# A new order table for a linear-attention and feed-forward kernel on one core

## The chip, the core and the metric

The kernel runs on one core of one Trainium2 chip. The core has five engines that work side by side, each through its own queue, strictly in order: TensorE (PE in the profile) multiplies matrices, VectorE (DVE) and ScalarE (ACT) do elementwise work, GpSimd (POOL) does slower elementwise work and issues the two weight loads, and the SyncE queue (SP) issues all other DMA transfers. The metric is the device time of one execution in microseconds (us). An instruction that waits for a semaphore holds up everything behind it on its engine.

## What is computed

The inputs are q, k, v and a complex decay a, each for 4 batches, 8 heads, 768 steps and 48 features, in float32. The attention part is a recurrence over time, cut here to what matters:

```python
scale = minimum(mag, 0.999) / (mag + 1e-06)          # mag = |a|
for t in range(S):
    S_re, S_im = ar*S_re - ai*S_im + outer(k[t], v[t]), ar*S_im + ai*S_re
    y[t] = q[t] @ S_re
```

The heads are then put side by side (384 features), and each of the 3072 rows goes through a layer norm with a gain, a product with a 384 x 1536 matrix, a ReLU, a product with a 1536 x 384 matrix, and is added to its input:

```python
xn = (x - mu) / sqrt(var + 1e-06) * g_ln
out = x + maximum(xn @ w_ch1, 0.0) @ w_ch2
```

## The kernel before, in words

Time is cut into chunks of 128 steps; two chunks make a pair. There are 24 chunks (n = 0 to 23) and 12 pairs (P = 0 to 11), three pairs to a batch. The recurrence is turned into matrix products: the cumulated logarithm of the decay and its cumulated angle come from products with triangular matrices, q and k are scaled and turned by them, and inside a chunk the result is a masked product.

For each pair, by the names that the code uses: `are`, `aim`, `k`, `q`, `vf` are loads on SP (lines 400 and 448). `ln`, `iv`, `r`, `r2`, `u`, `l`, `lc` make the log of the magnitude; `dec` is its cumulated sum on PE (line 484), and `e`, `en` its exponentials on ACT. `th`, `ph`, `sin`, `cos` (with `qt` or `abs`) do the same for the angle. `ke`, `qe` multiply k and q by the exponentials, in two chunks each (m = 0, 1), and `ks`, `qs` multiply them by cosine and sine (a = 0, 1); pair 0 is in two halves of the heads. `v` copies the values to bfloat16.

For each chunk: `kT`, `qT` turn ks and qs over on PE (eight transposes each, line 598) and `ksT`, `qsT` copy them from PSUM to SBUF on DVE or ACT; where the table gives `ksT` or `qsT` to SP (line 603) a DMA turns them over and the PE part is left out. `am` (line 621) is the masked product of both, `atm` applies the mask on DVE, `gm` and `G` carry the state, `y` is the chunk's output (lines 682 and 685), `bn` its mean and variance, `x` the centred row, `xtr` and `xT` turn it over (lines 719, and 725 for the DMA form), `xr` keeps it for the residual.

For each pair the feed-forward part: `mm1` (line 752, six half-groups of six matmuls of 256 columns), `relu`, then for each chunk `mm2` (line 776, three groups of four matmuls of 384 columns), `ot` or `oa` with `ot` for the scaling and residual, and `st` for the store. The weights come once: `wl.0` (line 365) and `wl.1` (line 367) are issued by POOL, and `wc` (line 381) multiplies the nine blocks of the first by the gain on DVE.

At the start, 71 matmuls named `warm` (lines 806 and 810) read a constant and their results are used by nobody. 15 `tab` operations load tables of ACT's functions.

The order of the work is written out by hand in one table, `PLAN`: each token is an operation, its engine (P, A, V, G, S) and, where it uses PSUM, the first of its eight banks. `Graph.run` emits the operations in that order, so the table fixes the order on every engine. A token may end in `@other`: then the operation also waits until `other` is done. The code calls this "turns at the shared port". Rings of buffers (`RINGS`) say how many pairs or chunks may be in flight of each tile.

Of the kernel before, what the change touches and what calls it, by code (L numbers as in the profile page):

```python
# [42 lines left out]
are.1.0:S ue:G are.0.0:S are.0.1:S pad.qs.1:G pad.ks.2:G aim.1.0:S ident:G car0.0:G pad.qs.2:G aim.0.0:S tab.log.0:A  # L43
ln.1.0:A uec:G aim.0.1:S qrow:G iv.1.0:A uth:V are.2.0:S zdec:G@uth ln.0.0:A car0.1:G@uth ln.0.1:A pick:G@uth iv.0.1:A
k.0.0:S pad.qs.0:G iv.0.0:A q.0.1:S r.1.0:V q.0.0:S r.0.1:V tab.trig.1:A th.1.0:A r.0.0:V r2.0.1:V th.0.1:A r2.1.0:V
vf.0.1:S th.0.0:A r2.0.0:V warm.w0:P0 warm.w1:P0 warm.w2:P0 warm.w3:P0 warm.w4:P0 warm.w5:P0 warm.w6:P0 warm.w7:P0
warm.w8:P0 warm.w9:P0 warm.w10:P0 warm.w11:P0 warm.w12:P0 warm.w13:P0 warm.w14:P0 warm.w15:P0 warm.w16:P0 warm.w17:P0
warm.w18:P0 warm.w19:P0 warm.w20:P0 warm.w21:P0 warm.w22:P0 warm.w23:P0 warm.w24:P0 warm.0:P0 warm.1:P0 warm.2:P0
ph.0.1:P0 pad.ks.0:G@r2.0.0 aim.2.0:S ph.0.0:P6 car.0.1:V0 mask:G@r2.0.0 car.0.0:V6 pad.ks.1:G@r2.0.0 k.0.1:S
warm.w25:P1 warm.3:P1 warm.4:P1 ph.1.0:P2 tab.log.2:A u.0.1:A u.0.0:A l.0.1:V k.1.1:S u.1.0:A l.0.0:V lc.0.1:V  # L50
ln.2.0:A car.1.0:V2 q.1.1:S warm.w26:P1 warm.w27:P1 warm.5:P1 warm.6:P1 dec.0.1:P1 lc.0.0:V l.1.0:V en.0.1:A1
warm.7:P4 dec.0.0:P7 e.0.1:A1 iv.2.0:A q.1.0:S lc.1.0:V qe.0.1.0:V warm.w28:P4 warm.w29:P4 warm.8:P4 warm.9:P4
warm.10:P4 dec.1.0:P4 en.0.0:A7 uthc:V vf.0.0:S e.0.0:A7 r.2.0:V e.1.0:A4 warm.11:P1 warm.12:P1 dps.0:P7 are.3.0:S
r2.2.0:V en.1.0:A4 ke.0.0.0:V u.2.0:A gln:S ke.0.1.0:V qe.0.0.0:V aim.3.0:S qe.1.0.1:V qe.1.0.0:V k.1.0:S l.2.0:V
tab.trig.3:A sin.0.0:A6 sin.0.1:A0 warm.w30:P1 warm.w31:P1 warm.w32:P1 warm.w33:P1 warm.13:P1 warm.14:P1@en.1.0
warm.w34:P1 warm.w35:P1 warm.w36:P1 warm.w37:P1 warm.15:P1 warm.16:P1@qe.0.0.0 warm.w38:P1 warm.w39:P1 warm.w40:P1
warm.17:P1 warm.18:P1 warm.19:P1 warm.20:P1 qt.0.0:P6 qs.0.0.1:V sin.1.0:A2 qt.0.1:P0 ks.0.0.1:V vf.1.1:S lc.2.0:V
# [11 lines left out]
rstd.1:G xT.3:V2 tab.log.6:A u.3.0:A ke.2.0.0:V mm1.1.0.1:P2 relu.0.0:A0 l.3.0:V mm1.1.1.0:P4 relu.0.2:A6 mm1.1.1.1:P4  # L69
ks.2.0.0:V lc.3.0:V mm1.1.2.1:P0 ks.2.0.1:V relu.1.1:A4 qe.2.0.0:V dec.3.0:P6 rstd.0:A qs.2.0.0:V mm1.1.0.0:P2  # L70
en.3.0:A6 qs.2.0.1:V kT.5:P4 vf.2.1:S e.3.0:A6 qT.4:P5 mm1.1.2.0:P0 ksT.5:A4 qsT.4:V5 qT.5:P6 are.5.0:S G.3:V
relu.1.2:A0 kT.4:P5 qsT.5:V6 mm2.0.0:P4 are.6.0:S ksT.4:V5 ln.4.0:A am.5:P6 mm2.0.1:P4 iv.4.0:A atm.5:V6 aim.5.0:S
mm2.0.2:P4 relu.1.0:A2 am.4:P0 r.4.0:V q.3.0:S mm2.1.0:P5 atm.4:V0 r2.4.0:A v.2:G@r.4.0 mm2.1.1:P5 q.3.1:S mm2.1.2:P5
xr.2:G@r.4.0 u.4.0:A ot.0:V4 mm2.2.0:P6 ln.5.0:A l.4.0:V st.0:S gm.4:P2 mm2.2.1:P6 iv.5.0:A G.4:V2 y.4:P0 lc.4.0:V
ln.6.0:A mm2.2.2:P6 xr.3:V k.3.0:S bn.4:V0 xr.1:G@xr.3 dec.4.0:P2 iv.6.0:A r.5.0:G@xr.3 k.3.1:S x.4:V0 y.5:P1 e.4.0:A2
dps.3:P4 bn.5:V1 xtr.4:P0 vf.3.1:S mm2.3.0:P7 oa.2:A6 xT.4:V0 en.4.0:A2 vf.3.0:S x.5:V1 mm2.3.1:P7 qe.3.0.0:G ot.1:V5
r2.5.0:A xtr.5:P0 k.4.1:S mm2.3.2:P7 rstd.2:G xT.5:V0 qe.3.0.1:V mm1.2.0.0:P0 u.5.0:A aim.6.0:S qs.3.0.0:V
mm1.2.0.1:P0 qs.3.0.1:V q.4.1:S mm1.2.2.1:P2 ke.3.0.0:V ot.3:V7 mm1.2.2.0:P2 k.4.0:S tab.trig.7:A th.4.0:A ke.3.0.1:V
qT.6:P5 relu.2.2:A2 ks.3.0.0:V ph.4.0:P6 q.4.0:S decc.3:V4 ks.3.0.1:V relu.2.0:A0 mm1.2.1.0:P2 l.5.0:V k.5.0:S kT.7:P4
abs.4.0:A6 qsT.6:V5 v.3:G@l.5.0 dps.4:P1 car.4.0:A6 kT.6:P0 vf.4.0:S ksT.7:V4 sin.4.0:A6 r.6.0:G@l.5.0 qT.7:P5  # L80
ksT.6:V0 mm1.2.1.1:P2 are.8.0:S decc.4:A1 qsT.7:V5 th.5.0:A am.6:P6 st.1:S gm.6:P4 relu.2.1:A2 ot.2:G ph.5.0:P0
atm.6:V6 are.7.0:S th.6.0:A ke.4.0.0:G am.7:P2 G.6:V4 y.6:P5 sin.5.0:A0 mm2.5.0:P6 atm.7:V2 ke.4.0.1:G vf.4.1:S
cos.4.0:A mm2.5.1:P6 qe.4.0.1:G bn.6:V5 mm2.5.2:P6 abs.5.0:A0 q.5.0:S ks.4.0.1:V y.7:P2 cos.5.0:A q.5.1:S lc.5.0:V
gm.7:P4 mm2.4.0:P7 ks.4.0.0:V x.6:A5 bn.7:V2 mm2.4.1:P7 xr.5:G@ks.4.0.0 r2.6.0:A aim.7.0:S G.7:V4 qe.4.0.0:G@ks.4.0.0
mm2.4.2:P7 x.7:V2 k.7.0:S dec.5.0:P0 qs.4.0.0:V xtr.6:P2 qs.4.0.1:V xtr.7:P3 st.2:S kT.9:P4 tab.log.8:A e.5.0:A0
xT.6:V2 v.4:G@qs.4.0.1 qT.8:P5 xT.7:V3 en.5.0:A0 ksT.9:V4 mm1.3.1.0:P2 ksT.8:S xr.4:V ln.7.0:A qT.9:P4 qsT.8:V5
qe.5.0.0:G@xr.4 mm1.3.1.1:P2 u.6.0:A qsT.9:V4 aim.8.0:S mm1.3.2.0:P0 relu.3.1:A2 l.6.0:V am.9:P4 st.3:S mm1.3.2.1:P0
iv.7.0:A k.5.1:S lc.6.0:V atm.9:V4 mm1.3.0.0:P2 qe.5.0.1:G@lc.6.0 ln.8.0:A mm1.3.0.1:P2 relu.3.2:A0 r.7.0:G@lc.6.0
ot.4:V7 dec.6.0:P4 vf.5.1:S ot.5:V6 relu.3.0:A2 gm.8:P7 ph.6.0:P0 G.8:V7 rstd.3:G vf.6.1:S en.6.0:A4 qs.5.0.1:V
am.8:P2 r2.7.0:V st.4:S e.6.0:A4 mm2.6.0:P6 qs.5.0.0:V iv.8.0:A mm2.6.1:P6 atm.8:V2 k.6.0:S xr.7:G@qs.5.0.0 mm2.6.2:P6  # L90
u.7.0:A xr.6:G@qs.5.0.0 vf.5.0:S abs.6.0:V0 r.8.0:G@qs.5.0.0 y.9:P4 y.8:P2 k.6.1:S bn.9:V4 mm2.7.0:P3 q.7.1:S bn.8:V2
gm.9:P7 tab.trig.9:A sin.6.0:A0 mm2.7.1:P3 ke.5.0.1:G gs.9:V7 are.9.0:S x.9:A4 mm2.7.2:P3 ot.6:V6 ke.5.0.0:G th.7.0:A
qT.11:P4 x.8:V2 st.6:S dps.6:P5 G.9:G cos.6.0:A car.6.0:V0 qT.10:P2 q.6.0:S qsT.11:V4 xtr.8:P6 ke.6.0.0:G xtr.9:P7
ph.7.0:P0 xT.8:A6 xT.9:V7 th.8.0:A qsT.10:V2 q.6.1:S mm1.4.1.1:P6 l.7.0:V decc.6:A5 car.7.0:A0 mm1.4.0.1:P4 abs.7.0:A0
ks.5.0.0:V mm1.4.0.0:P4 r2.8.0:V aim.9.0:S sin.7.0:A0 ks.5.0.1:V mm1.4.1.0:P6 relu.4.0:A4 lc.7.0:V kT.10:P1 ot.7:V3
q.7.0:S ke.6.0.1:G@lc.7.0 kT.11:P2 relu.4.1:A6 ksT.10:V1 k.7.1:S mm1.4.2.0:P4 ksT.11:V2 st.5:S am.10:P0 ks.6.0.1:V
am.11:P6 atm.10:V0 dec.7.0:P2 v.5:G@ks.6.0.1 tab.log.10:A rstd.4:A mm1.4.2.1:P4 ln.9.0:A vf.6.0:S xr.8:G@ks.6.0.1
# [749 lines left out]
```

## Time and profile before

| what | value |
|---|---|
| three runs | 187.19, 187.59, 187.84 us; median 187.59 |
| profiled execution: span from its first to its last instruction | 185.6 us |
| median of the runs less that span | 2.0 us |
| TensorE clock granted | full in all 40 slices |
| busy: PE, DVE, ACT, POOL | 177.0, 157.7, 154.6, 99.8 us |

The page gives no time of the profiled execution beside its span. In the profile a line such as `24.53 12.18 DMA w1b<-in_moe_w_ch_dram` is a piece of the chain that ended last: its start in us, its length, and what it was. In a timeline the columns are start, length, engine, line of the code, operation, output and inputs, shapes and count; in square brackets stands the idle time of the engine ahead of it and what ended it. In a list of groups the two numbers behind the bar are the busy time in us and the mean length of one in ns.

### The profile page before, as it was taken

Reading aid. Unit: us, or ns where it says so; the run is one execution under the profiler, and the core shown is the slowest. Engines: PE = TensorE matmul, PEld = TensorE weight load, DVE = VectorE, ACT = ScalarE, POOL = GpSimd, SP = SyncE. Lnnn points to the kernel's source line nnn. Section 1 sums busy time; section 2 is a strip of 40 time slices with the busy share of each in tenths; the row PEclk is TensorE's granted clock in tenths of the full one; section 3 lists DMA queues with packets and bytes.
Section 4 is the critical chain, followed back from the end, with each engine's and each line's share of the span. In section 5 each row is a group of like instructions: output and inputs, shape, how many; then the busy total and the mean of one; then the engine's idle time right before and its main releaser. Section 6 shows DMA issues by size and latency. Waiting matters only on the chain.

```text
span 185.6 us, 5131 instructions
## 1 busy us (share of the span) xinstructions
PE 177.0 (95%) x2029; PEld 139.0 (75%) x2029; DVE 157.7 (85%) x302; ACT 154.6 (83%) x218; POOL 99.8 (54%) x128
## 2 busy tenths in 40 slices
...
## 3 DMA queue, kind: packets, MB, share of 16 engines
...
## 4 chain that ended last, share of the span: by engine, by line
PE 59%; ACT 14%; DMA 10%; DVE 10%; issue 3%; SPq 2%; DVEq 0%
PE banks L752 22%; PE banks L776 19%; DMA w1b<-in_moe_w_ch_dram 7%; PE banks L598 4%; PE banks L621 4%; ACT L815 3%; PE banks L484 2%; DMA are<-in_a_re_dram 2%; DMA k<-in_k_dram 2%; ACT are L457 2%; PE banks L682 2%; DVE l L473 1%; ACT h L764 1%; PE banks L685 1%; ACT w L455 1%
## 5 line engine op out<-in xcount | busy, mean ns | idle before, releaser
L752 PE MATMUL banks<-xT,w1b 128*128 128x256 bf16 x432 | 52.7, 273 | 0.2
L776 PE MATMUL banks<-w2b,h 128*128 128x384 bf16 (+2 forms) x300 | 52.5, 319 | 0.0
L752 PEld LDWEIGHTS <-w1b 128*128 128x128 bf16 x432 | 45.8, 114 | 1.7 <-DVE w1b L381 0.4
L764 ACT ACTIVATE h<-banks 128x1024 bf16<-128x1024 f32 x33 | 32.8, 1022 | 8.3 <-PE banks L752 8.1
L776 PEld LDWEIGHTS <-h 128*128 128x128 bf16 x300 | 26.9, 97 | 14.1
L292 DVE TENSOR_TENSOR atm<-banks,mask 128x1024 bf16<-128x1024 f32 x24 | 28.9, 1218 | 1.9 <-PE banks L621 1.6
L815 ACT ACT_TABLE_LOAD x15 | 19.2, 1283 | 1.0 <-PEq L831 0.8
L292 POOL TENSOR_TENSOR ke<-k,en 128x384 bf16<-128x384 f32 x14 | 12.7, 916 | 8.3 <-DVE l L476 5.6
L292 POOL TENSOR_TENSOR qe<-q,e 128x384 bf16<-128x384 f32 x15 | 13.7, 916 | 6.1 <-DVE w1b L381 1.9
L292 POOL TENSOR_TENSOR ks<-ke,trig 128x768 bf16<-128x768 bf16 x7 | 11.4, 1643 | 6.4 <-PE banks L752 4.2
L621 PE MATMUL banks<-qsT,ksT 128*128 128x128 bf16 x192 | 14.6, 219 | 0.1
L410 POOL TENSOR_SCALAR v<-vf 128x768 bf16<-128x768 f32 x7 | 5.8, 831 | 16.0 <-DVE r L292 8.9
L810 PE MATMUL banks<-u_e 128*128 128x512 f16 x42 | 11.7, 418 | 2.2 <-POOL u_e L320 2.2
L292 POOL TENSOR_TENSOR r<-aim,are 128x768 f16<-128x768 f32 x7 | 12.7, 1817 | 1.9 <-ACT x L699 1.5
L709 POOL TENSOR_SCALAR xr<-x,mv 128x384 f32<-128x384 bf16 x16 | 9.3, 586 | 8.1 <-PE banks L752 3.3
L621 PEld LDWEIGHTS <-ksT 128*128 128x128 bf16 x192 | 12.0, 98 | 1.8 <-DVE ksT L289 0.5
L692 DVE BATCH_NORM_STATS2 stats<-banks 128x6 f32<-128x384 f32 x24 | 13.4, 556 | 0.1
L682 PE MATMUL banks<-v,atm 128*128 128x48 bf16 x192 | 12.1, 183 | 0.3 <-ACT x L699 0.2
L473 DVE SCALAR_TENSOR_TENSOR l<-r,w 128x768 f16<-128x768 f16 (+1 forms) x13 | 11.5, 892 | 0.9 <-ACT r L469 0.7
L791 DVE SCALAR_TENSOR_TENSOR ot<-banks,rstd,xr 128x384 f32<-128x384 f32 (+2 forms) x18 | 10.5, 590 | 2.0 <-PE banks L776 1.6
L455 ACT ACTIVATE w<-are 128x768 f32<-128x768 f32 (+1 forms) x13 | 10.2, 790 | 2.3 <-DMA are<-in_a_re_dram 2.3
L682 PEld LDWEIGHTS <-atm 128*128 128x128 bf16 x192 | 11.0, 96 | 1.2 <-DVE atm L292 0.2
...
## 6 DMA issues: line engine op xcount, KB each, us to landing
...
```

What stands on the lines that cost most here:

```text
L292: {"DVE": nc.vector, "POOL": nc.gpsimd}[eng(name)].tensor_tensor(**kw)
L455: add(f"ln.{X}", lambda S_=S_: act(out=S_("w"), in_=S_("are"), func=AF.Ln), needs=[f"are.{X}"], uses=[("are", P), ("w", P)])
L473: nc.vector.scalar_tensor_tensor(out=S_("l"), in0=S_("r2"), scalar=0.5, in1=S_("w"), op0=ALU.mult, op1=ALU.add)
L621: nc.tensor.matmul(ps[:, h], lhsT=T("ksT", n)[:, h], rhs=T("qsT", n)[:, h], start=True, stop=True)
L682: nc.tensor.matmul(ps[:, h], lhsT=T("atm", n)[:, h], rhs=T("v", P)[:, c, h], start=True, stop=nfirst)
L692: nc.vector.bn_stats(out=T("stats", n), in_=bank(f"y.{n}")[:, 0:DM])
L752: nc.tensor.matmul(ps[:, jj], lhsT=w1b[:, dc, ts(gi, JG * C)].rearrange("k (p j) -> k j p", j=JG)[:, jj], rhs=T("xT", P)[:, dc].rearrange( ...
L764: act(out=dst, in_=src, func=AF.Relu)
L776: nc.tensor.matmul(bank(f"o.{N}")[:, ws], lhsT=T("h", P)[:, j, ts(c, C)], rhs=w2b[:, j, ws], start=(j == 0), stop=(j == NJ - 1))
L791: nc.vector.scalar_tensor_tensor(out=o, in0=bank(f"o.{N}")[:, ws], scalar=T("rstd", P)[:, ds(c, 1)], in1=xs, op0=ALU.mult, op1=ALU.add)
L810: g.add(f"warm.w{i}", lambda i=i: nc.tensor.matmul(bank(f"warm.w{i}"), lhsT=u_e[:, 0, 0], rhs=u_e.rearrange("p c j t -> p (c j t)"), start ...
L815: g.add(f"tab.{nm}.{i}", lambda tab=tab: nc.scalar.preload_act_table_set(tab))
```

## The change

Only `PLAN` is replaced; no operation's code is touched. The new table holds the same computation with these differences, counted token by token:

- 90 operations that stand in both tables are on another engine. Of the elementwise multiplications, 8 `ke` and 4 `qe` go from DVE to POOL and 4 `qe` the other way; 5 `ks` go each way; 3 `qs` go to DVE. 2 `r` go from DVE to POOL; of `x`, 8 go from DVE to ACT and 3 back; the rest are single ones of `v`, `xr`, `G`, `r2`, `relu`, `xT`, `ksT`, `qsT`, `rstd`, `ot`, `abs`, `decc`. DVE has 266 operations for 275, POOL 116 for 107, ACT 210 for 209.
- `ksT.21` and `xT.21` are no longer DMA transposes; so `kT.21` (eight transposes) and `xtr.21` (three) come in on PE.
- 66 tokens have an `@` for 47.
- The order is new on every engine, SP's loads and the `warm` matmuls among it, and so are many banks. The number of `warm` matmuls and of table loads is the same. The PE operations that stand ahead of the first `mm1` are the same set.

The diff, cut to the rows around the first weight load and the first feed-forward products:

```diff
--- before.py
+++ after.py
@@ -40,105 +40,106 @@
 PLAN = """
-cos.0.0:A6 ks.0.1.1:V warm.21:P1 warm.22:P1 qt.1.0:P2 qs.1.0.1:V cos.0.1:A0 vf.1.0:S dps.1:P5 qs.0.1.1:V cos.1.0:A2
-dec.2.0:P0 ks.0.1.0:V k.2.1:S ks.0.0.0:V decc.0:A7 qs.0.1.0:V kT.0:P6 decc.1:A5 qs.0.0.0:V th.2.0:A qs.1.0.0:V
-wl.0:G@qs.0.0.0 qT.0:P2 q.2.1:S v.0:V qT.1:P3 ksT.0:A6 qsT.0:V2 qT.2:P4 ke.1.0.0:G@v.0 k.2.0:S kT.1:P5 qsT.1:A3
...
-xT.1:A7 wc.1.0:V qt.3.0:P0 wc.1.2:V cos.2.0:A2 wl.1:G@xT.1 vf.2.0:S wc.0.0:V mm1.0.1.0:P6 wc.0.1:V cos.3.0:A0 bn.2:V5
-y.3:P3 aim.4.0:S mm1.0.1.1:P6 wc.0.2:V x.2:A5 wc.2.1:V wc.2.2:V mm1.0.0.1:P0 wc.2.0:V relu.0.1:A6 bn.3:V3
-qe.2.0.1:G@wc.2.0 xtr.2:P2 mm1.0.0.0:P0 xT.2:V2 x.3:V3 ke.2.0.1:G@wc.2.0 mm1.0.2.1:P6 gs.3:V4 xtr.3:P2 mm1.0.2.0:P6
...
+qt.1.0:P2 cos.0.1:A1 qs.1.0.1:V warm.w29:P5 warm.w16:P4 cos.1.0:A2 qs.0.1.0:V dec.2.0:P0 q.2.1:S qs.0.0.0:V ks.0.0.0:V
+th.2.0:A qT.0:P4 qs.1.0.0:V warm.9:P3 ks.0.1.0:V warm.11:P6 qT.2:P5 qsT.0:A4 ks.0.0.1:V wl.0:G@ks.0.1.0 kT.0:P7
+qsT.2:V5 k.2.0:S qT.1:P4 ksT.0:V7 ke.1.0.0:G kT.1:P2 are.4.0:S qsT.1:V4 warm.24:P7 am.0:P6 v.0:G tab.log.4:A ln.3.0:A
...
+wc.1.2:V xtr.1:P6 gm.3:P4 wc.1.0:V xT.1:A6 qt.3.0:P0 wc.1.1:V cos.2.0:A2 wc.0.2:V mm1.0.1.1:P6 wc.0.0:V are.5.0:S
+wl.1:G@wc.0.2 bn.2:V5 cos.3.0:A0 mm1.0.1.0:P6 wc.0.1:V x.2:A5 y.3:P3 wc.2.0:V aim.5.0:S wc.2.2:V relu.0.1:A6 xtr.2:P2
+wc.2.1:V mm1.0.0.0:P0 ke.2.0.1:G@wc.2.2 bn.3:V3 are.6.0:S mm1.0.0.1:P0 gs.3:V4 qe.2.0.1:G@bn.3 x.3:V3 mm1.0.2.1:P6
...
 """
```

More of the change, by code (lines that the diff above doesn't have):

```diff
@@ L42 @@
 PLAN = """
[L43 to L57, printed above, removed]
@@ L68 @@
-qe.2.0.1:G@wc.2.0 xtr.2:P2 mm1.0.0.0:P0 xT.2:V2 x.3:V3 ke.2.0.1:G@wc.2.0 mm1.0.2.1:P6 gs.3:V4 xtr.3:P2 mm1.0.2.0:P6
[L69 to L97, printed above, removed]
@@ L98 @@
-atm.11:V6 y.10:P0 qe.6.0.0:G e.7.0:A2 mm2.9.0:P1 k.8.0:S bn.10:V0 en.7.0:A2 qe.6.0.1:G ph.8.0:P6 q.8.1:S relu.4.2:V4
-u.8.0:A ks.6.0.0:G mm2.9.1:P1 are.11.0:S iv.9.0:A gm.10:P2 mm2.9.2:P1 G.10:V2 abs.8.0:A6 mm2.8.0:P3 qs.6.0.0:V x.10:A0
-xr.9:V y.11:P2 qs.6.0.1:V mm2.8.1:P3 bn.11:V2 qsT.13:S r.9.0:G@qs.6.0.1 xtr.10:P0 mm2.8.2:P3 x.11:V2 tab.trig.11:A
-sin.8.0:A6 kT.13:P4 ot.9:V1 are.10.0:S xT.10:A0 xtr.11:P2 qT.12:P5 ke.7.0.0:G th.9.0:A xT.11:V2 kT.12:P0 ot.8:V3
-k.8.1:S mm1.5.0.1:P6 cos.7.0:A qe.7.0.0:G ksT.13:V4 mm1.5.0.0:P6 st.8:S ksT.12:V0 cos.8.0:A v.6:G qsT.12:V5
@@ L138 @@
[L138 to L141 removed]
+ue:G are.1.0:S are.0.0:S are.0.1:S uth:V aim.1.0:S warm.w17:P5 uec:G warm.25:P7 aim.0.1:S warm.1:P4 warm.w32:P2
+aim.0.0:S pick:G@uth warm.w13:P5 are.2.0:S warm.w33:P5 tab.log.0:A ln.1.0:A warm.18:P1 ident:G warm.w37:P7 ln.0.0:A
@@ new lines @@
+G.4:V6 mm2.1.0:P1 vf.3.0:S decc.3:V5 xr.1:G bn.4:V0 dec.4.0:P2 r.5.0:G ot.0:V4 y.5:P6 e.4.0:A2 mm2.3.0:P5 st.0:S
+bn.5:V6 en.4.0:A2 k.3.0:S mm2.2.2:P7 x.5:V6 k.4.1:S x.4:A0 mm2.1.1:P1 k.4.0:S xr.3:V oa.2:A7 r2.5.0:V mm2.1.2:P1
+vf.3.1:S ln.6.0:A qe.3.0.1:V xtr.4:P4 xtr.5:P2 qe.3.0.0:G@r2.5.0 u.5.0:A mm2.3.1:P5 xT.5:V2 xT.4:V4 aim.6.0:S
+mm2.3.2:P5 iv.6.0:A ot.1:V1 ke.3.0.1:V mm1.2.2.0:P2 q.4.0:S qs.3.0.1:V mm1.2.0.0:P0 l.5.0:V mm1.2.0.1:P0 tab.trig.7:A
+th.4.0:A qs.3.0.0:V mm1.2.2.1:P2 ke.3.0.0:G@l.5.0 ot.3:V5 relu.2.0:A0 ph.4.0:P6 st.3:S rstd.2:G@qs.3.0.0 lc.5.0:V
@@ new lines @@
+relu.2.2:A2 st.1:S ks.3.0.0:V qT.6:P4 q.4.1:S ks.3.0.1:V qT.7:P0 sin.4.0:A6 ot.2:G@ks.3.0.0 qsT.6:V4 mm1.2.1.1:P2
+car.4.0:A6 qsT.7:V0 kT.6:P5 ke.4.0.1:G abs.4.0:A6 st.2:S mm1.2.1.0:P2 k.5.1:S ksT.6:V5 th.5.0:A ke.4.0.0:G@qsT.6
+aim.7.0:S kT.7:P4 q.5.1:S am.6:P6 relu.2.1:A2 ksT.7:V4 v.3:G@qsT.7 ph.5.0:P0 are.7.0:S atm.6:V6 cos.4.0:A r.6.0:G
+gm.6:P4 am.7:P2 sin.5.0:A0 vf.4.0:S G.6:V4 dps.4:P5 mm2.5.0:P6 abs.5.0:A0 atm.7:V2 ks.4.0.0:G gm.7:P4 q.5.0:S
+decc.4:A5 mm2.4.0:P7 th.6.0:A G.7:V4 y.6:P2 are.8.0:S y.7:P5 r2.6.0:A bn.6:V2 dec.5.0:P0 xr.4:G@G.7 cos.5.0:A bn.7:V5
@@ new lines @@
+qe.4.0.1:G mm2.4.1:P7 vf.4.1:S x.6:V2 x.7:A5 mm2.5.1:P6 qe.4.0.0:V mm2.4.2:P7 ks.4.0.1:V xtr.6:P3 qs.4.0.1:V
+mm2.5.2:P6 qs.4.0.0:V tab.log.8:A u.6.0:A xtr.7:P2 kT.9:P4 xT.6:V3 e.5.0:A0 xT.7:V2 qT.8:P5 ot.4:V7 mm1.3.1.0:P2
+en.5.0:A0 ksT.9:V4 qe.5.0.1:G st.4:S mm1.3.1.1:P2 ksT.8:S ln.7.0:A qsT.8:V5 xr.5:G@ksT.9 qT.9:P7 relu.3.1:A2 l.6.0:V
+mm1.3.2.1:P0 q.6.1:S mm1.3.2.0:P0 iv.7.0:A aim.8.0:S qsT.9:V7 qe.5.0.0:G@l.6.0 mm1.3.0.0:P2 ot.5:V6 relu.3.2:A0
+am.9:P4 lc.6.0:V st.5:S xr.7:V mm1.3.0.1:P2 ln.8.0:A vf.5.0:S v.4:G@lc.6.0 atm.9:V4 k.6.0:S ph.6.0:P0 relu.3.0:A2
```

121 lines of the change are left out of this document (77 added, 44 removed).

## The prediction, made before the changed kernel ran

> **What bounds the kernel now.** I read the stages first (busy time by engine, then granted clock, DMA share, GB/s), then the chain that ended last, then the timelines around its joints.
>
> ```profile
> core 0: us, PE busy (x) PEld busy (x) DVE busy (x) ACT busy (x) POOL busy (x), PEclk, DMA share, GB/s
> 0.00:37.48 37.48, 32.63 (x317) 20.01 (x318) 28.70 (x58) 33.90 (x53) 18.74 (x40) 1.00 0.99 216
> 37.48:182.02 144.54, 144.34 (x1712) 118.97 (x1712) 128.61 (x244) 120.67 (x166) 81.02 (x89) 1.00 0.88 186
> 182.02:185.60 3.58, 0.00 (x0) 0.00 (x0) 0.35 (x1) 0.00 (x0) 0.00 (x0) 1.00 0.33 112
> ```
>
> ```profile
> 24.53 12.18 DMA w1b<-in_moe_w_ch_dram
> 36.81 0.20 DVE w1b L381
> 37.08 0.36 DVE w1b L381
> 37.48 0.89 PE banks L752 x6
> ...
> 46.53 0.89 PE banks L598 x16
> ...
> 129.20 0.29 PE banks L579 x8
> ...
> 173.30 0.17 PE banks L719 x3
> ...
> 174.12 3.96 PE banks L752 x36
> 178.07 3.94 PE banks L776 x36
> ```
>
> The span falls into three parts. Up to 37.48 the kernel waits for the first weights: the load w1b is issued at 24.53, lands 12.18 us later, is scaled, and the first `mm1` starts. From there PE is busy 144.34 of 144.54 us at full clock. Then 3.58 us of last output and store. So the middle part is PE's sum of work, and DVE (128.61) and ACT (120.67) are under it. Is that PE working, or PE waiting with a matmul open? I went through PE's timeline group by group (487 groups from 37.48 to 177.91) and compared the distance of starts with the steps that the chain shows, 3.96/36 = 0.110 us for an `mm1` matmul and 3.94 us for 24 full-width `mm2` ones. Only four holes above 0.1 us appear, 0.78 us in all; the largest is here:
>
> ```profile
> 117.02 0.36 PE L579 MATMUL banks<-ident,e 128*48 128x1 bf16 x8
> 117.49 0.84 PE L752 MATMUL banks<-xT,w1b 128*128 128x256 bf16 x6
> ```
>
> Eight such matmuls take 0.29 us where the next follows at once (129.20 in the chain); here the next starts after 0.47. **The middle part has 0.2 us (by busy time) to 0.8 us (by holes) to give, no more.** A new order of the same work can gain beyond that only by an earlier first `mm1`.
>
> **Part one, PE's own work.** The set of PE operations ahead of the first `mm1` is the same in both tables, so nothing moves out of the middle part. `kT.21` and `xtr.21` come into it: eight transposes at 0.89/16 = 0.056 us are 0.45, three are 0.17. Sum **+0.6 us**. Nothing hides it, since PE has no holes; the DMA transposes that go were hidden already.
>
> **Part two, the start.** Two things must be ready: w1b with its scaling, and `xT.0`, `xT.1`.
>
> ```profile
> 24.53 0.99 POOL L365 DMA_DIRECT2D w1b<-in_moe_w_ch_dram  x1 [12.65 <-DVE qs L292]
> 37.46 0.83 POOL L367 DMA_DIRECT2D w2b<-in_moe_w_ch_dram  x1 [1.79 <-ACT xT L287]
> ```
>
> ```profile
> w1b<-in_moe_w_ch_dram POOLq DMA_DIRECT2D x1, 1152.0 KB, 12.2
> w2b<-in_moe_w_ch_dram POOLq DMA_DIRECT2D x1, 1152.0 KB, 11.3
> ```
>
> ```profile
> 20.51 1.57 ACT L521 ACTIVATE trig<-banks 128x384 bf16<-128x384 int16 x3
> 21.96 1.60 ACT L532 ACTIVATE trig<-banks 128x384 bf16<-128x384 int16 x3
> ...
> 36.68 0.47 ACT L287 COPY xT<-banks 128x384 bf16<-128x384 bf16 x1
> ...
> 39.11 0.58 ACT L699 ACTIVATE x<-banks,mv 128x384 bf16<-128x384 f32 x1 [0.54 <-DVE mv L693]
> ```
>
> POOL issues the load when `qs.0.0.0` is done; the new table hangs it on `ks.0.1.0`. DVE gives `ke.0.0.0` and `qe.0.0.0` to POOL, but that does not carry through: the six sines and cosines of pairs 0 and 1 on ACT, 20.51 to about 23.5, stand behind an unbroken row of the same ACT work in both tables. After `cos.1.0`, the last, the new DVE order has `qs.1.0.0` (0.5 by the rows of its shape below, less the overlap with its neighbours) and `ks.0.1.0` (a half, 0.3), and the load goes at about 24.35: 0.2 us earlier. SP's loads of this time are the same ones with a few exchanged; those of pair 2 and the angles of pair 4 share the DMA engines with w1b as before. I take 12.18 again, so the first `mm1` starts at about 37.3. **-0.2 us.** Bounds: w1b as fast as w2b, 11.3, would give 0.9 more, but then `xT.1` ends first: walking DVE's new order (two copies for each of q and k, `atm.0`, `atm.1`, `ks.1.0.1`, `bn.0`, three copies, `G.1`, `atm.2`, `bn.1`) puts `xT.1`'s end at 36.65 for 37.15, so no more than 0.7 in all. The other way, 0.5 later if more of SP's loads get ahead of it.
>
> **Part three, the first feed-forward products.**
>
> ```profile
> 38.61 1.48 PE L752 MATMUL banks<-xT,w1b 128*128 128x256 bf16 x12
> ```
>
> Before, `y.3` stands between the first half-group (37.48, 6 x 0.110) and this row, so it takes 0.4. The new order puts `xtr.2` one half-group (0.65 us) closer to the start: after two half-groups and `y.3`, 1.3 + 0.4 us behind 37.3, at 39.0. It needs `x.2`, which is made behind the same five scalings of w1b and `bn.2` as before; its row ends at 39.69, moved with w1b to 39.5. PE waits 0.5 us, where this stage had one of the four holes, 0.2: **+0.3 us**, bounds 0 and 0.6. The second weight load hangs on the fourth scaling for `xT.1`, some 0.3 us later; the first `mm2` moves 0.9 us later by the PE operations counted between it and the first `mm1`, so the load stays covered by 0.6 us. If it took 12.2 us it would cost 0.3.
>
> **Part four, the moved operations.** They lie beside PE's work. From the groups of one shape:
>
> ```profile
> L292 POOL TENSOR_TENSOR r<-aim,are 128x768 f16<-128x768 f32 x7 | 12.7, 1817 | 1.9 <-ACT x L699 1.5 <-ACT are L457 0.3
> L292 POOL TENSOR_TENSOR ke<-k,en 128x384 bf16<-128x384 f32 x14 | 12.7, 916 | 8.3 <-DVE l L476 5.6 <-ACT r L469 1.8 <-ACT en L488 0.8
> L292 POOL TENSOR_TENSOR ks<-ke,trig 128x768 bf16<-128x768 bf16 x7 | 11.4, 1643 | 6.4 <-PE banks L752 4.2 <-issue 2.2
> L473 DVE SCALAR_TENSOR_TENSOR l<-r,w 128x768 f16<-128x768 f16 x11 | 10.5, 954 | 0.1
> L709 POOL TENSOR_SCALAR xr<-x,mv 128x384 f32<-128x384 bf16 x16 | 9.3, 586 | 8.1 <-PE banks L752 3.3 <-DVE xr L709 2.4 <-DVE ks L292 1.3
> L292 DVE TENSOR_TENSOR ks<-ke,trig 128x768 bf16<-128x768 bf16 x15 | 8.3, 554 | 0.0
> L410 POOL TENSOR_SCALAR v<-vf 128x768 bf16<-128x768 f32 x7 | 5.8, 831 | 16.0 <-DVE r L292 8.9 <-DVE l L473 4.4 <-DVE ks L292 1.4
> L476 DVE TENSOR_SCALAR l<-l 128x768 f16<-128x768 f16 x11 | 3.9, 354 | 0.1
> L709 DVE TENSOR_SCALAR xr<-x,mv 128x384 f32<-128x384 bf16 x8 | 3.3, 413 | 0.0
> L292 POOL TENSOR_TENSOR r<-r 128x768 f16<-128x768 f16 x1 | 1.5, 1457 | 0.0
> L292 POOL TENSOR_TENSOR G<-gt,dec 128x384 bf16<-128x384 f32 x2 | 1.7, 828 | 1.3 <-DVE gt L292 1.3
> ```
>
> DVE falls by some 6 us in the middle part and POOL rises by 11 of 144; neither sets the end, so this relief is worth nothing by itself. What counts is whether the two get in each other's way. POOL and DVE take turns:
>
> ```profile
> 102.03 1.81 POOL L292 TENSOR_TENSOR r<-aim,are 128x768 f16<-128x768 f32 x1 [1.55 <-ACT x L699]
> ...
> 105.56 0.83 POOL L410 TENSOR_SCALAR v<-vf 128x768 bf16<-128x768 f32 x1
> ```
>
> ```profile
> 101.34 0.55 DVE L292 TENSOR_TENSOR qs<-qe,trig 128x768 bf16<-128x768 bf16 x1
> ...
> 106.38 0.55 DVE L292 TENSOR_TENSOR qe<-q,e 128x384 bf16<-128x384 f32 x1
> ```
>
> While POOL works from 102.03 to 106.39, DVE does only operations that read PSUM or one small tile; its next product of two SBUF tiles starts at 106.38. In the whole trace none of DVE's products runs beside more than a sliver of a large POOL operation. So these operations share one turn. From the first `mm1` of pair 4 to that of pair 7 (about 90 to 130 us) I count what needs it. Before: POOL 11 `ke`/`qe`, 4 `ks`/`qs`, 2 `r`, 3 `v`, 4 `xr` = 25.1; DVE 13 products at 0.554 (`ks`, `qs`, `ke`, `qe`, `r2`), 4 `l`, 4 `lc`, 3 `xr` = 13.7; together 38.8, beside 39.9 us of PE work. After: POOL 11 `ke`/`qe`, 4 `ks`/`qs`, 3 `r`, 1 `r2`, 2 `v`, 5 `xr`, 2 `G` = 29.8; DVE 11 products, 3 `l`, 4 `lc` = 10.4; together 40.2, beside 39.6 of PE. Elsewhere the sum stays under PE's over any such length, but for some ten us after 60. So the turn is full there, and an operation that comes late finds no room. Cost between 0 (POOL's `xr`, `v` and `r` have slack) and 2.2 us (below); I take 0, as PE waited only 0.3 at the fullest places of before.
>
> The Trainium skill, SBUF — State Buffer, section "SBUF: two separate sides", states that DVE and GpSimd share one pair of SBUF ports as an exclusive lock held for the whole instruction, by which a DVE operation with two SBUF inputs fully blocks against a GpSimd one that reads SBUF. The trace agrees (106.38 against 106.39). By that rule the stage's load is the 40.2 above, without it DVE's busy time alone; it speaks against moving products to an engine that holds the lock 0.916 us for 0.55.
>
> **Sum.** 185.6 + 0.6 - 0.2 + 0.3 = 186.3 us of span. The median of the three runs, 187.59, is 2.0 above the profiled span; so **188.3 us**.
>
> **Rivals.** (A) The shared turn becomes the bound from 90 to 130. Before, 38.8 us of turns went into 40.4 us, so 1.6 were lost between turns. The same loss on 40.2 makes 41.8, 2.2 over PE's 39.6: 190.5 us. For: the count, and 66 waits on `@` for 47. Against: fewer hand-overs (48 operations for 49), and not every operation is urgent. It decides once turns and hand-overs exceed PE's work. (B) The end on the other side: the load w1b comes through faster. Then `xT.1` ends the start, 0.7 earlier, and if the 0.8 us of holes go too: 185.6 - 0.7 + 0.6 - 0.8 = 184.7, or 186.7 us; with only the start, 187.5. For: w2b took 11.3. Against: DMA share 0.99 up to 37.48, the same loads beside it. (C) The holes close (DVE has 6 us more room) and the rest cancels: 186.3 - 0.8 = 185.5, 187.5 us, no change. (D) The change does not do what it says: an order that bears scattered load landings finds no landing to bear, because no hole of PE ends on a load after 37.48. That speaks for C or the forecast, not for a gain.
>
> **How the numbers follow.** The forecast with its own range 187.7 to 189.2: 0.45. A: 0.17. B: 0.18. C and D with no change: 0.20. About 0.3% (0.56 us) is what a measurement of this kernel can tell from no change: under 187.03 is faster, over 188.15 slower. Faster: most of B, 0.17. Same: C, the rest of B and a quarter of the forecast, 0.32. Slower: the rest, 0.51. The range leaves out half of B's lower end and A's upper tail: 186.8 to 190.3.
>
> **What would show it.** Right: first `mm1` at 37.0 to 37.5; PE busy for all but about 1 us from there to the last `mm2`, in a stretch of about 145.3; 264 + 8 transposes at line 598; a hole ahead of `xtr.2` near 39. A would show as PE holes between 90 and 130 with POOL's products ahead of them. Wrong: a first `mm1` before 36.6, or a middle part under 144.5, which would mean that PE had waited inside busy time where I saw none.

## The result, and the profile after

The changed kernel takes **189.27 us** (median of 15 runs, 188.50 to 190.88), the kernel before 187.59 (15 runs, 186.99 to 189.60): a ratio of 1.0083 (95% interval 1.0054 to 1.0113), slower. Its profiled execution spans 187.3 us for 185.6. In the new file each line of code has a number one higher (`mm1` is L753).

The stages of the changed kernel, cut like those of before at the first `mm1` and the last `mm2` (span, then busy us of PE, PEld, DVE, ACT, POOL, then clock, DMA share, GB/s):

```profile
0.00:38.08 38.08, 32.47 (x318) 20.69 (x319) 28.06 (x58) 33.09 (x53) 20.18 (x40) 1.00 0.97 209
38.08:183.62 145.54, 144.59 (x1724) 119.74 (x1723) 126.73 (x236) 122.22 (x167) 94.81 (x97) 1.00 0.87 184
183.62:187.28 3.66, 0.00 (x0) 0.00 (x0) 0.35 (x1) 0.00 (x0) 0.00 (x0) 1.00 0.21 69
```

The first `mm1` starts 0.60 us later, the stretch behind it is 1.0 longer, the tail 0.1: the 1.7 us of span. In the stretch PE's idle time rose from 0.2 to 0.95 us. I also summed PE's holes as in the prediction, from the distance of starts against the step of each width, now all those above 0.07 us: 1.36 us before, 1.90 after. Without them the stretch was 143.17 and is 143.64. So the account is **start +0.60, PE's work +0.47, holes +0.54, tail +0.08**. The line between work and holes is good to some 0.1 us, since it depends on the step that is taken for each width.

**The start.** From the timelines of the changed kernel, first DVE, then POOL, then ACT, then PE:

```profile
27.38 2.34 DVE L293 TENSOR_TENSOR atm<-banks,mask 128x1024 bf16<-128x1024 f32 x2
29.64 0.96 DVE L293 TENSOR_TENSOR ks<-ke,trig 128x768 bf16<-128x768 bf16 x1
...
34.76 0.55 DVE L693 BATCH_NORM_STATS2 stats<-banks 128x6 f32<-128x384 f32 x1
...
37.03 1.39 DVE L382 TENSOR_SCALAR w1b<-w1b,ngl 128x512 bf16<-128x512 bf16 x5
```

```profile
24.85 0.99 POOL L366 DMA_DIRECT2D w1b<-in_moe_w_ch_dram  x1 [4.25 <-DVE ks L293]
...
28.55 1.64 POOL L293 TENSOR_TENSOR ks<-ke,trig 128x768 bf16<-128x768 bf16 x1
```

```profile
35.62 0.58 ACT L700 ACTIVATE x<-banks,mv 128x384 bf16<-128x384 f32 x1 [0.25 <-DVE mv L694]
...
37.55 0.48 ACT L288 COPY xT<-banks 128x384 bf16<-128x384 bf16 x1
```

```profile
36.74 0.49 PE L529 MATMUL banks<-qrow,pick 1*128 1x384 f16 x2
37.17 0.34 PE L720 MATMUL banks<-ident,x 128*128 128x128 bf16 x3
```

```profile
w1b<-in_moe_w_ch_dram POOLq DMA_DIRECT2D x1, 1152.0 KB, 9.7
```

The load came in 9.7 us for 12.2, and landed at 34.51, 2.2 us earlier than before. Nobody used that: DVE came to its scaling only at 37.03. The last to be ready was `xT.1` at 38.03, made from `x.1`, which waited for DVE's `bn.1` (34.76). In DVE's row ahead of it `ks.1.0.1` lasts 0.96 for its normal 0.55, since POOL holds the shared turn with `ks.1.0.0` up to 30.19. And `x.1` is done at 36.20, but PE turns it over (`xtr.1`) only at 37.17, behind `y.2` and `qt.2.0`; the old table has `xtr.1` ahead of `qt.2.0`.

Part of the 0.60 belongs to this execution and not to the table: the load went at 24.85, but at 24.50 and 24.45 in e1 and e3 below, whose tables are the same up to the first `mm1`. From the issue of the load to the first `mm1` it takes 13.23 to 13.25 us with the new start (after, e1, e3), 12.95 in the kernel before and 12.82 or 12.83 in e4, e8 and e9, which have the old start. So the new chain is 0.3 to 0.4 us longer.

**The largest hole.** Timelines of DVE, POOL and PE of the changed kernel:

```profile
125.47 1.01 DVE L293 TENSOR_TENSOR ks<-ke,trig 128x768 bf16<-128x768 bf16 x2
126.40 2.00 DVE L293 TENSOR_TENSOR qs<-qe,trig 128x768 bf16<-128x768 bf16 x1
...
129.59 0.62 DVE L703 TENSOR_SCALAR x<-banks,mv 128x384 bf16<-128x384 f32 x1
```

```profile
126.16 1.82 POOL L293 TENSOR_TENSOR qs<-qe,trig 128x768 bf16<-128x768 bf16 x1 [0.94 <-DVE ks L293]
```

```profile
128.70 0.61 PE L599 MATMUL banks<-ident,qs 128*128 128x128 bf16 x8
130.26 0.34 PE L720 MATMUL banks<-ident,x 128*128 128x128 bf16 x3 [0.95 <-DVE x L703]
```

The new table lets `qs.8.0.1` on POOL wait for `ks.8.0.0`, the old one for `qs.8.0.0`. `ks.8.0.0` is the first of the two at 125.47; POOL is released 0.2 us ahead of DVE's own `qs.8.0.0`, and that lasts 2.00 us for 0.55. `bn.15` and `x.15` follow late, and `xtr.15` starts 1.11 us behind its place. **A blocked product shows as a long instruction, not as idle time.** So I compared each instruction with the usual length of its form: what is above it sums to 0.2 us on DVE before and 4.2 after, on POOL 1.4 and 7.8. The groups show it too; POOL's `ke` and `xr` were 916 and 586 ns before, and DVE's `qs`, at 623, stays at 0.0 us of idle time:

```profile
L293 POOL TENSOR_TENSOR ke<-k,en 128x384 bf16<-128x384 f32 x22 | 22.2, 1012 | 15.8 <-DVE l L474 3.5 <-ACT en L489 3.2 <-DVE xr L710 2.5
L710 POOL TENSOR_SCALAR xr<-x,mv 128x384 f32<-128x384 bf16 x15 | 9.9, 662 | 2.5 <-DVE l L474 2.5
...
L293 DVE TENSOR_TENSOR qs<-qe,trig 128x768 bf16<-128x768 bf16 x21 | 12.8, 623 | 0.0
```

**PE's work.** Two rows of its groups: 136 transposes by `kT` for 128 (`qT` has 136 in both tables), 63 by `xtr` for 60.

```profile
L599 PE MATMUL banks<-ident,ks 128*128 128x128 bf16 x136 | 10.0, 219 | 0.0
L720 PE MATMUL banks<-ident,x 128*128 128x128 bf16 x63 | 6.7, 220 | 0.9 <-DVE x L703 0.9
```

### The profile page after: what moved, and what is told of

It reads as the page before. It is cut to its first block, busy times and chain, and to the rows that moved or that the text cites. A ratio compares the mean times of both kernels' runs of the same rounds, so it can differ in the third digit from the quotient of the medians.

```text
span 187.3 us, 5185 instructions
## 1 busy us (share of the span) xinstructions
PE 177.1 (95%) x2040; PEld 140.4 (75%) x2040; DVE 155.1 (83%) x293; ACT 155.3 (83%) x219; POOL 115.0 (61%) x137
## 4 chain that ended last, share of the span: by engine, by line
PE 76%; DVE 10%; ACT 8%; DMA 2%; issue 1%; SPq 1%; DVEq 0%
PE banks L753 24%; PE banks L777 23%; PE banks L599 7%; PE banks L622 5%; DVE atm L293 3%; PE banks L504 3%; PE banks L485 3%; DMA are<-in_a_re_dram 2%; PE banks L683 2%; ACT L816 2%; PE banks L720 2%; PE banks L686 2%; PE banks L646 2%; PE banks L500 2%; ACT r L470 1%
## 5 line engine op out<-in xcount | busy, mean ns | idle before, releaser
L777 PE MATMUL banks<-w2b,h 128*128 128x384 bf16 (+2 forms) x300 | 53.8, 319 | 0.0
L753 PE MATMUL banks<-xT,w1b 128*128 128x256 bf16 x432 | 52.5, 273 | 0.0
L753 PEld LDWEIGHTS <-w1b 128*128 128x128 bf16 x432 | 45.8, 114 | 1.0 <-DVE w1b L382 0.3
L765 ACT ACTIVATE h<-banks 128x1024 bf16<-128x1024 f32 x33 | 33.3, 1022 | 10.5 <-PE banks L753 10.5
L293 POOL TENSOR_TENSOR ke<-k,en 128x384 bf16<-128x384 f32 x22 | 22.2, 1012 | 15.8 <-DVE l L474 3.5
L293 POOL TENSOR_TENSOR qe<-q,e 128x384 bf16<-128x384 f32 x15 | 14.4, 962 | 7.8 <-ACT e L489 3.4
L293 POOL TENSOR_TENSOR r<-aim,are 128x768 f16<-128x768 f32 x9 | 16.5, 1838 | 3.3 <-DMA aim<-in_a_im_dram 1.4
L811 PE MATMUL banks<-u_e 128*128 128x512 f16 x42 | 14.4, 436 | 2.2 <-POOL u_e L321 2.2
L792 DVE SCALAR_TENSOR_TENSOR ot<-banks,rstd,xr 128x384 f32<-128x384 f32 (+2 forms) x19 | 11.2, 590 | 6.2 <-PE banks L777 5.3
L293 DVE TENSOR_TENSOR qs<-qe,trig 128x768 bf16<-128x768 bf16 (+1 forms) x25 | 14.0, 579 | 0.0
L622 PEld LDWEIGHTS <-ksT 128*128 128x128 bf16 x192 | 12.2, 98 | 0.9
L293 POOL TENSOR_TENSOR ks<-ke,trig 128x768 bf16<-128x768 bf16 x7 | 11.9, 1699 | 0.1
L710 POOL TENSOR_SCALAR xr<-x,mv 128x384 f32<-128x384 bf16 x15 | 9.9, 662 | 2.5 <-DVE l L474 2.5
```

The lines of the kernel that those rows point to most:

```text
L293: {"DVE": nc.vector, "POOL": nc.gpsimd}[eng(name)].tensor_tensor(**kw)
L622: nc.tensor.matmul(ps[:, h], lhsT=T("ksT", n)[:, h], rhs=T("qsT", n)[:, h], start=True, stop=True)
L753: nc.tensor.matmul(ps[:, jj], lhsT=w1b[:, dc, ts(gi, JG * C)].rearrange("k (p j) -> k j p", j=JG)[:, jj], rhs=T("xT", P)[:, dc].rearrange( ...
L765: act(out=dst, in_=src, func=AF.Relu)
L777: nc.tensor.matmul(bank(f"o.{N}")[:, ws], lhsT=T("h", P)[:, j, ts(c, C)], rhs=w2b[:, j, ws], start=(j == 0), stop=(j == NJ - 1))
L792: nc.vector.scalar_tensor_tensor(out=o, in0=bank(f"o.{N}")[:, ws], scalar=T("rstd", P)[:, ds(c, 1)], in1=xs, op0=ALU.mult, op1=ALU.add)
```

## The experiments

The theory after the result: PE's work sets the stretch, the start is set by DVE's chain to `xT.1`, and the hole is a turn lost at one place. Rivals: the turns are too many for the stage (rival A of the prediction), or the two added transposes explain all. The kernel before gave 187.59, 187.49 and 187.59 us beside the three sets of runs (e1 to e4, e5 to e8, e9 to e11). Line numbers in their rows are shifted by a few, with the length of each table.

**e1: the one wait put back** (changed kernel)

```diff
-qs.8.0.1:G@ks.8.0.0
+qs.8.0.1:G@qs.8.0.0
```

> The changed kernel with one token altered: POOL's qs.8.0.1 waits for DVE's qs.8.0.0 (as in the kernel before) and no longer for ks.8.0.0. Theory (collisions at the shared turn): in the changed kernel POOL's 1.8 us multiplication gets in ahead of DVE's, which then lasts 1.995 us for 0.55 and ends in the 1.1 us hole of PE ahead of xtr.15. With the wait back, DVE's lasts 0.55, the hole goes, and the time falls by 0.8 to 1.1 us, to about 188.3 (from 189.3). Rival (PE's hole comes from the order around x.15 whatever the turn, or the slack is used up elsewhere): the hole stays over 0.6 us or moves, and the time stays within 0.3 us of 189.3.

188.75 us, ratio 1.0072 (1.0046 to 1.0098). The hole ahead of `xtr.15` is gone and `mm1.7.0.1` comes 92.65 us behind the first `mm1` for 93.6. But POOL and DVE, displaced by this 1 us, now meet elsewhere (DVE of e1, then POOL):

```profile
126.08 0.55 DVE L292 TENSOR_TENSOR qs<-qe,trig 128x768 bf16<-128x768 bf16 x1
...
135.63 1.89 DVE L292 TENSOR_TENSOR qs<-qe,trig 128x768 bf16<-128x768 bf16 x1
```

```profile
135.46 1.64 POOL L292 TENSOR_TENSOR ks<-ke,trig 128x768 bf16<-128x768 bf16 x1
```

That gives a hole of 0.47 ahead of `xtr.17`; one of 0.9 opens ahead of `am.20`, on a DMA transpose. The stretch is 146.0. So the wait caused the hole, and the repair here was **given back later**: the first `mm1` came 0.33 earlier with the same table, and still the last `mm2` ends at 183.75 for 183.62. The profiled span (187.0 for 187.3) is shorter only by its tail. The stage from 90 to 130 was not too full: one token changed, the same operations, 1 us less.

**e7: the same clash put into the kernel before**

```diff
+qs.8.0.1:G@ks.8.0.1
 qs.8.0.0:V
...
-qs.8.0.1:G@qs.8.0.0
```

On POOL `qs.8.0.1` thereby also comes ahead of `ke.10.0.1`, as in the new table.

> The kernel before with one operation moved: POOL's qs.8.0.1 comes ahead of ke.10.0.1 and waits for DVE's ks.8.0.1 only, so that it asks for the turn before DVE's qs.8.0.0. Theory: qs.8.0.0 lasts about 2 us for 0.55, and what hangs on DVE behind it comes up to 1.4 us later; PE gets a hole of 0.5 to 1.2 us near 128, and the time rises to 188.1 to 188.8. Rival (POOL waits and DVE does not, or the slack at that place takes it): 187.6 within 0.3.

188.67 us, ratio 1.0070 (1.0044 to 1.0096). DVE, POOL and PE of e7:

```profile
127.45 2.00 DVE L291 TENSOR_TENSOR qs<-qe,trig 128x768 bf16<-128x768 bf16 x1
...
130.50 0.61 DVE L701 TENSOR_SCALAR x<-banks,mv 128x384 bf16<-128x384 f32 x1
```

```profile
127.27 1.76 POOL L291 TENSOR_TENSOR qs<-qe,trig 128x768 bf16<-128x768 bf16 x1
```

```profile
129.14 0.61 PE L597 MATMUL banks<-ident,ks 128*128 128x128 bf16 x8
130.64 0.33 PE L718 MATMUL banks<-ident,x 128*128 128x128 bf16 x3 [0.89 <-DVE gt L291]
```

The same 2.00 us, a hole of 1.05, and 1.2 us on the median. (The profiled execution of e7 had a late start for another reason, told in the last section.) POOL getting in ahead of one product of DVE is enough: this is shown, in both tables.

**e5: a wait at every POOL product** (changed kernel): each product of POOL waits for the last product of DVE ahead of it in the table, 55 tokens altered, such as

```diff
-v.1:G
+v.1:G@ks.1.0.1
```

> The changed kernel with the turns written out for all of POOL's products: each waits for the last DVE product that stands ahead of it in the table (55 tokens altered, 104 waits for 66). Theory (the new table lost the turns: 4.2 us of DVE's time go into waiting inside instructions, up to 1.45 in one): DVE's lengthened products fall from 4.2 us to under 1.5, the 1.1 us hole of PE goes, and the time falls by 0.5 to 1.5 us, to 187.8 to 188.8. Rival (the turn is simply overfull, 40.2 us in 39.6, so that order does not help): POOL comes late instead, holes open elsewhere between 90 and 130, and the time stays or rises over 189.3.

188.81 us, ratio 1.0069 (1.0036 to 1.0103). No hole over 0.2 is left, the stretch is 144.94 for 145.54, and POOL's lengthening falls from 7.8 to 3.7 us. DVE's did not fall as expected; it stays at 4.7: where the table puts a POOL product ahead of a DVE one, DVE still waits for it inside its instruction, as here. So the sum of the lengthening alone makes no hole; it has to fall on the chain that PE waits for.

```profile
138.02 1.59 DVE L296 TENSOR_TENSOR ks<-ke,trig 128x768 bf16<-128x768 bf16 x1
```

The waits also fall in the start, where w1b is issued 0.5 later and the first `mm1` comes at 38.57, which takes 0.5 of the gain back. (This is from one profile; the start of the new table without these waits was 37.69 to 38.08 in three.)

**e6: no turns at all** (kernel before): all 47 `@` struck.

> The kernel before with all 47 waits for turns struck out, nothing else. Theory (products of DVE and POOL exclude each other, and the old order is fast because POOL lets DVE go first): DVE's lengthened products rise from 0.2 us to some 4 to 8, holes open in PE, and the time rises by 1 to 3 us, to 188.6 to 190.6. Rival (the waits cost as much as they save): 187.6 within 0.3.

208.50 us, ratio 1.1101 (1.1053 to 1.1149). The stages of e6:

```profile
0.00:44.55 44.55, 35.13 (x317) 22.39 (x318) 30.26 (x58) 35.21 (x54) 21.23 (x42) 0.92 1.02 227
44.55:203.73 159.18, 149.46 (x1712) 121.03 (x1712) 143.49 (x244) 120.91 (x165) 88.46 (x86) 0.98 0.75 156
```

The stretch grows by 14.6 us, with 14.3 of holes; DVE's instructions lengthen by 16.8 us in sum, POOL's by 11.7. The granted clock fell to 0.98 in the stretch as well; 0.02 of 159 us is 3.2 us, an estimate of the most that the clock alone can have cost. So all the `@` together are worth some 11 to 14 us of the stretch in the old order; I can't part the two further. The other 7 us are at the start, from POOL's timeline:

```profile
8.82 0.99 POOL L361 DMA_DIRECT2D w1b<-in_moe_w_ch_dram  x1
29.82 0.98 POOL L288 TENSOR_TENSOR ke<-k,en 128x384 bf16<-128x384 f32 x1 [20.01 <-DMA k<-in_k_dram]
```

Without its `@` the weight load goes out at 8.82, ahead of part of the loads of pair 0 and of k, q and v of pair 1. SP's issues behind it come 6 to 7 us later, and POOL's first product, which needs k of pair 1 (issued at 25.09, for 18.52 in the kernel before), waits until 29.82. Of that token the wait is no turn but holds the load back.

**e2: `ks.1.0.1` moved behind `bn.0`** (changed kernel), out of POOL's way

```diff
-ks.1.0.1:V
 gm.0:P5
...
 bn.0:V0
+ks.1.0.1:V
 kT.2:P4
```

> The changed kernel with one operation moved on DVE: ks.1.0.1 stands behind bn.0 and no longer ahead of it. Theory (the start is set by DVE's chain to xT.1, and 0.4 us of it is ks.1.0.1 waiting for POOL's ks.1.0.0): ks.1.0.1 lasts 0.55 for 0.96 us, xT.1 and the first product of the feed-forward part come 0.3 to 0.4 us earlier (37.7 for 38.08), and the time falls by 0.3 to 0.4 us, to about 188.9. Rival (the start is set by the weight load or by ACT): the first product stays at 38.1 and the time at 189.3.

189.95 us, ratio 1.0123 (1.0093 to 1.0154): a miss. DVE and PE of e2:

```profile
30.61 0.53 DVE L292 TENSOR_TENSOR ks<-ke,trig 128x768 bf16<-128x768 bf16 x1
```

```profile
31.29 0.61 PE L598 MATMUL banks<-ident,ks 128*128 128x128 bf16 x8 [0.77 <-DVE ks L292]
```

The product is short again, but `kT.2` needs it and starts at 31.29 for 30.75; `bn.1` and `xT.1` follow, and the first `mm1` comes at 38.53. `ks.1.0.1` stands on the chain itself; the 0.4 us of its wait were not to be had by moving it away.

**e4: the old start, the new table behind it**: the old table up to its first `mm1`, then the rest in the new order.

> All of the old order and engines up to the first mm1, then the new table for all that is left. Theory (the start costs 0.6 us: first mm1 at 38.08 for 37.48): the first mm1 is back at 37.5 and the time falls by 0.6 us, to about 188.7, with the hole of 1.1 us ahead of xtr.15 still there. Rival (the loss is all in the middle, and the late start would be caught up there): 189.3. Rival (the faster landing of the first weights in the changed kernel, 9.7 us for 12.2, is worth something): slower than 189.3 by some tenths.

188.66 us, ratio 1.0063 (1.0036 to 1.0089). The first `mm1` is back at 37.31. The hole at `xtr.15` stays (1.11), and at the seam between the tables a new one of 0.56 opens ahead of `xtr.3`: POOL's `qe.2.0.0` starts at 38.27 and a scaling of w1b lasts 1.1 for 0.36. Of the gain of 0.8 at the start nothing is left at the last `mm2`, which ends at 183.81 for 183.62; the span (187.0 for 187.3) is shorter only by its tail.

**e9: e4 with the turns of e5 behind the seam**

> The old table up to the first mm1, the new one behind it, and behind it each POOL product waits for the last DVE product ahead of it in the table, the scalings of w1b counted among those (49 waits set). If start, lost turns and PE work are the whole account: first mm1 at 37.4, a stretch of 144.5 + 0.6 of PE work with no hole over 0.3, a span of 185.6 to 186.3, a median of 187.5 to 188.2. If the lost turns only move on, as they did in the two earlier repairs, a stretch of 146 or more and a median of 188.6 again.

188.39 us, ratio 1.0052 (1.0023 to 1.0081). Its middle stage:

```profile
37.26:182.89 145.63, 145.20 (x1724) 119.47 (x1723) 127.80 (x236) 122.11 (x167) 90.62 (x96) 1.00 0.86 183
```

A span of 186.2, within the expectation; the median is 0.2 over it, and one hole over 0.3 is left, the seam's 0.56. Without holes the stretch is 143.65, as after (143.64) and in e5 (143.62): the 0.5 us of PE's work that the new table adds stays in whatever is done about its waits. This is the best of the new table, and it is 0.8 over the kernel before.

**e3: `ksT.21` by DMA again** (changed kernel)

```diff
-kT.21:P3
+ksT.21:S
...
-ksT.21:A3
```

> The changed kernel with ksT.21 again a DMA transpose: eight transposes leave PE, one copy leaves ACT. Theory (PE is busy without a break, so each matmul more costs its own length): 0.45 us less, 188.8. Rival (PE has idle time inside its busy time): 189.3 within 0.2. If the DMA lands after the time at which am.21 is due (slack 0.5 us by the changed kernel's trace) a hole ahead of am.21 takes part of the gain.

190.37 us, ratio 1.0150 (1.0120 to 1.0180). PE of e3:

```profile
154.57 0.82 PE L752 MATMUL banks<-xT,w1b 128*128 128x256 bf16 x6
157.57 0.62 PE L621 MATMUL banks<-qsT,ksT 128*128 128x128 bf16 x8 [2.18 <-DMA ksT<-ks]
```

The expected 188.8 did not come: there is a hole of 2.35 us ahead of `am.21`; without it the stretch is 145.1, 0.44 less than after, as eight transposes should give. In the new order `ks.10.0.0` is done at 151.5, in the old at 143.4. So the two added groups of transposes cost their 0.5, but the new order as it stands needs the first of them: put back on the DMA at this place, it comes too late.

**e8: more work for PE** (kernel before): 34 products of 512 columns, whose results nobody uses, spread over the stretch.

> The kernel before with 34 matmuls of 512 columns more on PE, which read a constant and whose results nobody uses, put ahead of the products of the chunks that are turned over by DMA (chunks 8 to 23). Theory (PE is working all the time from the first mm1, and a matmul more costs its own length wherever it stands): 34 x 0.2165 = 7.4 us more, 195.0, within 0.7. Rival (PE has idle time that its busy time hides): 2 us or more less than that.

194.77 us, ratio 1.0401 (1.0346 to 1.0457). The middle stage of e8:

```profile
37.31:189.02 151.71, 151.65 (x1747) 122.47 (x1746) 129.47 (x243) 120.92 (x166) 80.49 (x89) 1.00 0.85 180
```

7.4 us of work were added, and the stretch grew by 7.2, as expected. There is no slack on PE that would hide such work.

**e10 and e11: less work for PE** (kernel before): `ksT.12`, `ksT.13`, `qsT.12`, `qsT.14` given to the DMA; in e11 `qsT.10`, `qsT.11` too. Of e10:

```diff
+ksT.13:S ksT.12:S
 x.10:A0
...
 qsT.13:S
+qsT.12:S
...
-kT.13:P4
...
-qT.12:P5
```

> The old table with four more transposes given to the DMA: ksT.12, ksT.13, qsT.12 and qsT.14, so that kT.12, kT.13, qT.12 and qT.14 leave PE. Theory (PE's own work sets the stretch): the inputs of these four are done 6 to 10 us before the product that reads them, a DMA transpose lands 3.4 us after its issue, so 4 x 0.45 = 1.8 us go: stretch 142.7, median 185.7. Rival (the DMA queue has no room there: share 0.96 to 1.00): loads behind them on SP come late or the transposes land late, a hole ahead of am.12 or at pair 10, and the median stays at 187.5 or rises.

> As the kernel with four, and qsT.10 and qsT.11 by DMA too, issued when qs.5 is done (about 84 us, needed at 94.7). Theory: 6 x 0.45 = 2.7 us less than before, stretch 141.9, median 184.9. Rival: in this stage the DMA share is 1.00 and the loads behind them feed pairs 6 and 7, so they come 2.7 us later on SP and a hole opens between 95 and 110; the gain over the kernel with four is then 0 or a loss.

e10: 188.95 us, ratio 1.0063 (1.0027 to 1.0098). e11: 192.58, ratio 1.0245 (1.0190 to 1.0300). PE of e10, then its middle stage:

```profile
119.28 0.61 PE L620 MATMUL banks<-qsT,ksT 128*128 128x128 bf16 x8 [0.34 <-DMA qsT<-qs]
...
123.58 0.62 PE L620 MATMUL banks<-qsT,ksT 128*128 128x128 bf16 x8 [1.07 <-DMA ksT<-ks]
```

```profile
38.37:184.45 146.08, 143.46 (x1681) 117.24 (x1680) 127.52 (x239) 120.98 (x166) 82.01 (x89) 1.00 0.92 189
```

PE's work did go: without its holes the stretch is 141.44 for 143.17, 1.73 of the 1.78 expected. But the holes grew from 1.36 to 4.64, so that the stretch became 1.5 longer: at `am.14` and `am.15` where PE waits for the transposes, and where `xT.11` and `xT.13` come late. In e11 they are 7.22, with 2.3 ahead of `am.12`. The rival held: from 100 to 120 the DMA has no pause (the stage view counts a share of 1.08 in e10 and 1.14 in e11, for 0.94 before), and on the queue of SP the transposes of e10 are issued one behind the other, 1.4 to 2 us apart. The old table's choice of which transposes PE makes has no gain left at these six. No version here beat the kernel before.

## Why the prediction was right

It said slower, 188.3, and 189.27 was measured, in its range. Its span of 186.3 was 1.0 short. Of the 1.7 us that the span grew, the prediction's reasons cover only PE's work, 0.5; that the direction held although the start came out with the wrong sign is in part luck, and the range was wide enough to hold no change as well. Step by step:

| step of the prediction | predicted | measured |
|---|---|---|
| PE's work | +0.6 | +0.5 |
| the start | -0.2 | +0.6 (between profiles +0.2 to +0.8) |
| hole ahead of `xtr.2` | +0.3 | 0 |
| the moved operations | 0 (0 to 2.2) | +0.5 |
| tail | 0 | +0.1 |

- **What bounds.** That PE's own work sets the stretch is shown by adding: 7.4 us added cost 7.2 (e8). Taking away shows less. Apart from the holes the stretch shrank by 0.44 and 1.73 where 0.45 and 1.78 were taken (e3, e10), which says that the work is gone; as a whole it grew in both, since the transposes came late by DMA.
- **The start: the step that failed.** "DVE's new order puts `xT.1`'s end at 36.65 for 37.15" was wrong by 1.4 us. The walk used lengths of free instructions and put each one behind its neighbour on DVE. It began too early: the load was to go at 24.35 and went at 24.85 (0.5; 0.1 to 0.15 in e1 and e3). It left out that `ks.1.0.1` would stand against POOL's `ks.1.0.0` (0.4), and that the chain runs through PE's order as well: `qt.2.0` now stands ahead of `xtr.1` (0.43). These three make 1.3 of the 1.4. With `xT.1` late, the load no longer mattered: rival B's cause came (9.7 us, 2.5 faster), and its gain didn't. Even with the old start the load hardly set the first `mm1`: in e4, e8 and e9 it took 10.8 to 11.2 us for 12.2 before, and the first `mm1` came only 0.2 earlier. In other profiles the new start gave 37.75 (e1) and 37.69 (e3), the old one 37.31 (e4, e8) and 37.26 (e9), so that part is sure in its sign and 0.2 to 0.8 in size.
- **The hole ahead of `xtr.2`**: 0.15 us at 39.8 where 0.5 was expected, because the first `mm1` came 0.8 later than predicted and `x.2` only 0.4 (39.90 for 39.5); the hole of 0.2 of the kernel before is gone.
- **The moved operations**: the sign of rival A was there, a hole between 90 and 130 with POOL's product ahead of it, at half its price. But its cause was another. A said that turns and hand-overs exceed PE's work in the stage; e1 changes no operation and takes the hole away, e5 has the same operations and no hole over 0.2, and e7 puts the same hole where the turns sum to 38.8. The count of the load did not tell this. Nor did the relief of DVE come: in the middle part its busy time fell by 1.9 us for the 6 expected, and POOL's rose by 13.8 for 11, since time spent blocked counts as busy. What did was in the diff: an `@` that names an earlier product than the DVE product that must go first. The Trainium skill, SBUF — State Buffer, section "SBUF: two separate sides", states that whichever of the two engines starts first holds the shared ports for its whole instruction. The traces agree: POOL started 0.2 us ahead, and DVE's product ended 0.42 us behind POOL's, 2.00 us long for 0.55 (after and e7).
- **Rival D** (no landing to bear) holds in so far as no hole over 0.3 us in the changed kernel ends on a load. Whether the new order bears later landings better was not tried.
